# Attention with bit-shifted exponentials: GpSimd's shifts as packed 64-bit integer adds, two of three there, and other GpSimd work on VectorE

## The chip, the cores and the metric

The kernel runs on one core of a Trainium2 chip. Its engines run side by side, each with its own instruction stream in a fixed order: TensorE (PE in the profile; PEld are its weight loads), VectorE (DVE), ScalarE (ACT), GpSimd (POOL) and SyncE (SP), which issues nearly all DMAs. They meet through semaphores. The metric is the time of one execution in microseconds on the device; "the time" of a kernel is the median of several executions.

## The reference, cut to what matters

Inputs are bf16. S = 2048 rows, D = 512, 32 heads of 16, F = 1376.

```
def _A_ref(x, wqkv, wo):                       # attention
    qkv = (x @ wqkv).reshape(B, S, 3, 32, 16).transpose(2, 0, 3, 1, 4)
    q, k, v = qkv[0], qkv[1], qkv[2]
    scores = einsum("bhqd,bhkd->bhqk", q, k) * 16 ** -0.5
    o = einsum("bhqk,bhkd->bhqd", softmax(scores), v)
    return o.transpose(0, 2, 1, 3).reshape(B, S, D) @ wo

def _B_ref(x, w1, b1, w2, b2):                 # MLP over the row axis
    h = _layernorm(x)
    u = gelu(einsum("bsd,sf->bdf", h, w1) + b1)
    return (einsum("bdf,fs->bds", u, w2) + b2).transpose(0, 2, 1)

xn = _layernorm(x)
return x + _A_ref(xn, A_wqkv, A_wo) + _B_ref(xn, B_w1, B_b1, B_w2, B_b2)
```

So the input is normalised once, the attention works on that, and the MLP normalises it a second time.

## The kernel before

**Tiling.** Queries are cut into four blocks of 512, heads into eight groups of four. For each of 32 blocks (a query block with a group of heads), 16 key tiles of 128 and two halves of the group, there is one *n*: 1024 in all. For each n two matmuls (L691, 32 rows, 512 columns each) write scores into a slot of two PSUM banks; there are three slots. Then 128x1024 exponentials go into one of 28 buffers in SBUF (`pT`, 20 of them, and the space of the input `x_sb`, 8). Then the buffer is multiplied with V (L754), in groups of four matmuls of 256 columns, summed up in one PSUM bank. V carries a column of ones, so the same sum gives the softmax's denominators.

**Two ways to an exponential.** On ScalarE it is one `activation` (L715). On VectorE it is approximate: `dexp_spec` (L726) adds a bias to the scores and writes them as int16, whose bits, read as bf16, are a straight-line approximation of the exponential. Three copies of it, with 22, 58 and 94 added to the int16 bits (`SHIFTS`, written by `shift_spec`, L731), are further terms of a sum which is nearer to the true curve. The four terms are multiplied with V one after the other, the last with a scaled copy of V, `VM`, which `vm_scale` (L569) makes. An n that VectorE takes therefore costs one instruction at L726, three at L731 and four groups of matmuls at L754; one that ScalarE takes costs one instruction at L715 and one group.

**What sets the order.** The program text is made by a planner (`Sched` and the loop from L1201) with a modelled duration for each operation: `EXP_I, EXP_L` = 0.903, 1.03 for ScalarE's exponential, `P1_I, P1_L` = 1.13, 1.22 for VectorE's, `TS_I, TS_L` = 0.335, 0.42 for a shift on VectorE and `SH_I, SH_L` = 1.02, 1.08 for one on GpSimd (the first figure is until the next instruction, the second until the result). It repeatedly takes the candidate that can start first by the model and appends it to its engine's stream. What it fixed is the order on the chip, whatever the durations are there. It also decides which n go to VectorE: only while fewer than `D_FLY` = 3 such n have shifts still to be placed, while at least 8 buffers are free, and while VectorE's backlog is at most `D_BACK` = 0.5.

**Shifts.** The first of the three (k = 0) may go only to GpSimd until the scores run out; the second and third may go to either. The planner treats some operations of VectorE and GpSimd as users of one port (`port=True`, `port_time`): by its model they do not run at the same time. In the program a GpSimd operation waits by semaphore for the last such operation of VectorE ahead of it; in the other direction there is no semaphore.

**Other work on GpSimd.** Small operations of the first layernorm (L478, L480); the statistics of the second one (`ln2_stats`, L508 to L512) and its scaling of the 16 row tiles (`ln2_norm`, L516), both issued from the generator `h_work` in the main loop; `vm_scale`; and in each pair of blocks' epilogue two products of the head outputs with the reciprocal denominators (L981), 128x256 each.

**Around it.** The first block's 32 n go through a prologue of 16 periods, in which all exponentials are ScalarE's, and in which layernorm, transposes and the first projections run. During the main loop TensorE also computes the projections of later heads, the MLP (`ut`, `fin`, L784) and the output projection, and VectorE copies their results out of PSUM. ScalarE's gelu (L888) runs once.

Of the kernel before, what the change touches and what calls it, by code (L numbers as in the profile page):

```python
# [9 lines left out]
BF16 = mybir.dt.bfloat16  # L10
I16 = mybir.dt.int16
F32 = mybir.dt.float32

# [44 lines left out]
DMA_L = 3.5  # L58
SH_I, SH_L = 1.02, 1.08
D_LAST = 31  # L60
# [238 lines left out]
def bass_parallel_sum__softmax_full_mha__mixer_token_mlp__prompt_kernel(  # L299
# [18 lines left out]
    with ExitStack() as es:  # L318
# [196 lines left out]
        def ln2_norm(t):  # L515
            sc.add("pool", lambda e: e.tensor_scalar(xn_sb[:, t, :], xn_sb[:, t, :], mv[:, t, 3:4], 1.0, ALU.mult, ALU.mult),  # L516
                   reads=[("xn", t), ("mv", t)], writes=[("xn", t)], cost=(0.67, 0.75))

# [47 lines left out]

        def vm_scale(tiles, T):
            t0_, n = tiles[0], len(tiles)
            sc.add("pool", lambda e: e.tensor_scalar(  # L569
                vm_kh[:, t0_:t0_ + n, 8 * T:8 * T + 8, :], v17_kh[:, t0_:t0_ + n, 8 * T:8 * T + 8, :], CM, 1.0, ALU.mult, ALU.mult),  # L570
                reads=[("V", t, T) for t in tiles] + [("Vone",)], writes=[("VM", t, T) for t in tiles],
                cost=(0.62, 0.7))

# [130 lines left out]
        def buf_keys(i):  # L704
            return [("pT", i)] if i < NPB else [("pT", i), ("x", 2 * (i - NPB)), ("x", 2 * (i - NPB) + 1)]
# [23 lines left out]

        def shift_spec(eng, w, o, k):  # L730
            return dict(eng=eng, fn=lambda e: e.tensor_scalar(  # L731
                buf_i(o), buf_i(w), float(SHIFTS[k]), 1.0, ALU.add, ALU.mult),
                reads=[("pT", w)], writes=buf_keys(o), name="sh", port=True,
                cost=(SH_I, SH_L) if eng == "pool" else (TS_I, TS_L))

# [91 lines left out]
        def task_vt(T, j):  # L827
            tiles = list(range(4 * j, 4 * j + 4))
            for i, t in enumerate(tiles):
# [14 lines left out]
                reads=[("bank", EX_BANK)], writes=[("V", t, T) for t in tiles])]  # L844
            yield "call", lambda: (vm_scale(tiles, T), have.add(("v", T, j)))

# [92 lines left out]
        def task_epilogue(b):  # L939
# [39 lines left out]
            for h in range(2):  # L979
                cs = slice(256 * h, 256 * h + 256)  # L980
                yield "pool", [dict(eng="pool", fn=lambda e, cs=cs: e.tensor_tensor(  # L981
                    oT[0:m, qb % 2, T, cs], oC32[0:m, tb_, cs], denb[0:m, tb_, cs], ALU.mult),
                    reads=[("oC32", tb_, x, c, a) for x in es_ for c in range(4) for a in range(2)] +
                          [("denb", tb_, x, r) for x in es_ for r in range(4)],
                    writes=[("oTc", qb % 2, T), ("oTh", h)], port=True, cost=(0.68, 0.74))]
            yield "call", lambda: oT_done.add((qb, T))
# [79 lines left out]
        for period in range(NKT):  # L1066
# [10 lines left out]
            if period in VM_AT:  # L1077
                j = VM_AT.index(period)
                vm_scale(list(range(4 * j, 4 * j + 4)), 0)

        late_consts()
# [32 lines left out]
        hgen = h_work()  # L1114
        next_n = BN
# [3 lines left out]
        cur_ext = None  # L1119
        frees = [g_gelu]  # L1120
        pv_block = 0
        pv_open = True
        free_slots = [0, 1, 2]
        next_h = 0.0

# [72 lines left out]
        last_n = None  # L1198
        step_gen(g_gelu)
        fin_next = 0  # L1200
        while True:  # L1201
# [52 lines left out]
            if hgen is not None:  # L1254
                pl.append((max(sc.free["pool"], next_h), 2, "h", None, 0.67))
            pl = [z for z in pl if max(dve_port, sc.free["dve"]) - z[0] >= z[4] - PORT_SLACK]
# [51 lines left out]
            if not cands:  # L1308
                pl = [z for z in ([] if not sh_jobs else [(0, 0, "shd", (sh_jobs[0], shift_spec("dve", sh_jobs[0]["w"], sh_jobs[0]["o"], sh_jobs[0]["k"])))])]
                pl += [(0, 0, "gen", g) for g in frees if g["cur"] and g["cur"][0] == "pool"]  # L1310
                if hgen is not None:
                    pl.append((0, 0, "h", None))
# [7 lines left out]
            if kind == "h":  # L1320
                if next(hgen, "end") == "end":
                    hgen = None
            elif kind == "exp":
                n, sp_ = what
# [4 lines left out]
            elif kind == "dexp":  # L1329
# [74 lines left out]
            if cur_ext is None:  # L1404
                for i, (rel, due, nm, gen, need) in enumerate(ext_tasks):
                    if rel > next_n:
                        continue
                    if need and need[0] == "ut" and (need[1] != len(u_begun) or hgen is not None):
                        continue
# [73 lines left out]
```

## Time and profile before

| | |
|---|---|
| time, median of 5 runs | 715.37 us (713.55 to 716.51) |
| the profiled execution's own time | 713.55 us |
| its span from first to last instruction | 711.8 us |
| TensorE's granted clock | 1.00 in every stage |
| ScalarE's exponentials, L715 | 733 (522 into `pT`, 211 into `x_sb`) |
| VectorE's exponentials, L726 | 291 (201 and 90) |
| shifts on VectorE, L731 | 572 (284 + 131 + 111 + 46), 0.44 to 0.46 us each |
| shifts on GpSimd, L731 | 301 (149 + 73 + 59 + 20), 1.044 to 1.046 us each |
| head products on GpSimd, L981 | 32, 0.735 us each |
| second layernorm's scaling on GpSimd, L516 | 16, 0.720 us each |
| V scaling on GpSimd, L569 | 16, 0.662 us each |

From 40 to 690 us, the main loop, the engines are busy for 634.9 (TensorE), 616.7 (VectorE), 646.3 (ScalarE) and 354.9 us (GpSimd) of 650. A row of the profile gives busy time, mean length of one, and the idle time of the engine just before them with what ended it. Lengths overlap: an instruction's row reaches until its result is written, while the next one has begun; the distance from start to start is what an engine can do.

### The profile page before, as it was taken

To read this page: it belongs to the slowest core of one execution; us is meant where nothing else is said; L and a number is where in the kernel's file an instruction comes from. 1 tells how busy PE (TensorE), PEld (TensorE's weight loads), DVE (VectorE), ACT (ScalarE), POOL (GpSimd) and SP (SyncE) were. 2 spreads that over 40 slices of the span, in tenths; PEclk is the share of its full clock that TensorE was granted. 3 is DMA by queue.
4 is the path that set the end of the run, shared out by engine and by line. 5 is a ranking of instruction groups with operands and counts; after the bars stand their busy time and mean duration, and the time that the engine had idled before them with its cause. 6 is when DMAs were issued, how large, how long until landed. Compare 5 with 4: busy or idle time off the path is not lost.

```text
span 711.8 us, 28996 instructions
## 1 busy us (share of the span) xinstructions
PE 688.2 (97%) x12716; PEld 309.8 (44%) x12716; DVE 666.0 (94%) x1093; ACT 690.8 (97%) x752; POOL 383.6 (54%) x420
## 2 busy tenths in 40 slices
PE   8998999999999999999999999999999999999997
PEld 4544444444545444444444434444443434443443
DVE  7967999998999999999999999999999999999997
ACT  5999999999999999999999999999999999999994
POOL 5567554563545556464554554645554555645653
PEclk9999999999999999999999999999999999999999
DMA  7130022121202112221222211112221112212111
GB/s 209 29 74 20 21 46 43 27 42 25 49 10 49 31 36 54 46 44 34 49 52 44 58 36 38 38 45 49 51 48 27 46 43 51 62 25 61 34 25 43
DMA packets 85727, 32.29 MB, mean 45 GB/s; under 512 B 67425, under 2 KB 85601, under 8 KB 85601
## 3 DMA queue, kind: packets, MB, share of 16 engines
q1 hardware_dynamic: 85168, 30.05, 18.6%
q8 instruction: 99, 1.62, 1.0%
q10 hardware_dynamic: 432, 0.39, 0.2%
q14 instruction: 28, 0.22, 0.1%
HBM read 21.76 MB, written 2.35 MB: 34 GB/s over the span
## 4 chain that ended last, share of the span: by engine, by line
PE 44%; ACT 39%; DVE 14%; issue 2%; POOL 1%; DMA 1%; SPq 0%; DVEq 0%
ACT pT L715 28%; PE ps L754 16%; PE ps L691 15%; ACT x_sb L715 10%; PE ps L784 10%; DVE pT L726 5%; DVE pT L731 4%; DVE x_sb L726 2%; DVE x_sb L731 1%; PE ps L833 1%; ACT gT_sb L888 1%; DVE OT L944 1%; PE ps L597 1%; DMA x_sb<-in_A_x_dram 0%; PE ps L528 0%
## 5 line engine op out<-in xcount | busy, mean ns | idle before, releaser
L715 ACT ACTIVATE pT<-ps 128x1024 bf16<-128x1024 f32 x522 | 514.4, 1124 | 3.2 <-PE ps L691 1.8
L691 PE MATMUL ps<-QT,KT 32*128 32x512 bf16 x2048 | 288.0, 384 | 10.6 <-ACT pT L715 5.7
L726 DVE TENSOR_SCALAR pT<-ps 128x1024 int16<-128x1024 f32 x201 | 244.3, 1215 | 10.0 <-PE ps L691 9.1
L754 PE MATMUL ps<-pT,V 128*32 128x256 bf16 x4576 | 243.3, 275 | 3.7 <-DVE V L842 1.2
L715 ACT ACTIVATE x_sb<-ps 128x1024 bf16<-128x1024 f32 x211 | 227.4, 1134 | 1.7 <-PE ps L691 1.4
L731 POOL TENSOR_SCALAR pT<-pT 128x1024 int16<-128x1024 int16 x149 | 155.8, 1046 | 124.9 <-DVE pT L731 82.9
L691 PEld LDWEIGHTS ps<-QT,KT 32*128 32x128 bf16 x2048 | 79.3, 91 | 192.1 <-ACT pT L715 90.7
L754 PEld LDWEIGHTS ps<-pT,V 128*32 128x32 bf16 x4576 | 109.8, 96 | 82.7 <-issue 59.1
L731 DVE TENSOR_SCALAR pT<-pT 128x1024 int16<-128x1024 int16 x284 | 121.7, 451 | 3.2
L754 PE MATMUL ps<-x_sb,V 128*32 128x256 bf16 x1848 | 115.7, 275 | 0.7 <-POOL x_sb L731 0.4
L726 DVE TENSOR_SCALAR x_sb<-ps 128x1024 int16<-128x1024 f32 x90 | 109.5, 1216 | 6.1 <-PE ps L691 5.8
L731 POOL TENSOR_SCALAR pT<-x_sb 128x1024 int16<-128x1024 int16 x73 | 76.2, 1044 | 62.4 <-DVE pT L731 47.8
L731 POOL TENSOR_SCALAR x_sb<-pT 128x1024 int16<-128x1024 int16 x59 | 61.6, 1044 | 53.3 <-DVE pT L731 37.0
L754 PE MATMUL ps<-pT,VM 128*32 128x256 bf16 x864 | 61.3, 275 | 1.6 <-POOL VM L569 1.5
L754 PEld LDWEIGHTS ps<-x_sb,V 128*32 128x32 bf16 x1848 | 47.4, 96 | 30.4 <-issue 22.7
L784 PE MATMUL ps<-gT_sb,wblk 128*32 128x512 bf16 (+1 forms) x704 | 58.4, 384 | 0.6 <-DVE Qall L806 0.6
L731 DVE TENSOR_SCALAR pT<-x_sb 128x1024 int16<-128x1024 int16 x131 | 57.2, 459 | 1.5
L784 PE MATMUL ps<-hx,wblk 128*32 128x512 bf16 x688 | 56.9, 382 | 0.0
L731 DVE TENSOR_SCALAR x_sb<-pT 128x1024 int16<-128x1024 int16 x111 | 50.0, 458 | 1.2
L981 POOL TENSOR_TENSOR oT<-oC,denb 128x256 bf16<-128x256 f32 (+1 forms) x32 | 23.5, 735 | 26.9 <-DVE pT L731 20.0
L731 POOL TENSOR_SCALAR x_sb<-x_sb 128x1024 int16<-128x1024 int16 x20 | 20.9, 1044 | 20.0 <-DVE pT L731 17.1
L754 PEld LDWEIGHTS ps<-pT,VM 128*32 128x32 bf16 x864 | 22.9, 96 | 14.0 <-issue 10.0
(103 smaller groups left out, 409.9 us busy)
## 6 DMA issues: line engine op xcount, KB each, us to landing
wblk<-in_B_w_dram SPq DMA_DIRECT2D x10, 512.0 KB, 4.5
wblk<-in_B_w_dram SPq DMA_DIRECT2D x16, 320.0 KB, 3.6
oC<-OT SPq DMA_DIRECT2D x248, 16.0 KB, 1.8
denb<-rden_scratch SPq DMA_DIRECT2D x124, 32.0 KB, 1.9
xr<-in_A_x_dram SPq DMA_DIRECT2D x16, 128.0 KB, 2.5
dcomp<-OT SPq DMA_DIRECT2D x124, 2.0 KB, 1.8
QT<-Qall SPq DMA_DIRECT2D x120, 16.0 KB, 1.8
out_dram<-osb SPq DMA_DIRECT2D x14, 128.0 KB, 2.0
```

What stands on the lines that cost most here:

```text
L597: sc.add("pe", lambda e: e.matmul(bank(bk), lhsT=src[:, 0:128], rhs=src, start=True, stop=True), reads=keys, writes=[("bank", bk)], cost=( ...
L691: specs.append(dict(eng="pe", fn=lambda e, r=r, bk=bk: e.matmul(bank(bk), lhsT=KT[32 * r:32 * r + 32, T, 128 * kt:128 * (kt + 1)], rhs=QT[ ...
L715: return [dict(eng="act", fn=lambda e: e.activation(buf(pbuf[n]), ps[:, s_ * 1024:(s_ + 1) * 1024], ACTF.Exp, scale=LN2_128), reads=[("ban ...
L726: return dict(eng="dve", fn=lambda e: e.tensor_scalar(buf_i(w), ps[:, s_ * 1024:(s_ + 1) * 1024], IBIAS, 0.0, ALU.add, ALU.max), reads=[(" ...
L731: return dict(eng=eng, fn=lambda e: e.tensor_scalar(buf_i(o), buf_i(w), float(SHIFTS[k]), 1.0, ALU.add, ALU.mult), reads=[("pT", w)], writ ...
L754: specs.append(dict(eng="pe", fn=lambda e, c=c, h=h, i=i, off=off: e.matmul(bank(PV_BANK)[32 * c:32 * c + 32, 256 * par:256 * par + 256], ...
L784: specs.append(dict(eng="pe", fn=lambda e, c=c, w=w: e.matmul(bank(EX_BANK)[32 * c:32 * c + w, :], lhsT=lhs_of(32 * c, 32 * c + w), rhs=rh ...
L833: specs.append(dict(eng="pe", fn=lambda e, ct=ct, c=c, i=i, t=t: e.matmul(bank(EX_BANK)[32 * c:32 * c + 32, 128 * i:128 * (i + 1)], lhsT=x ...
L888: yield "act", [dict(eng="act", fn=lambda e, ap=ap: e.activation(ap, ap, ACTF.Gelu_apprx_tanh), reads=[("gT", f) for f in fts], writes=[(" ...
L944: yield "pvev", [dict(eng="dve", fn=lambda e: e.tensor_copy(OT32[:, eb, :], bank(PV_BANK)), reads=[("bank", PV_BANK)], writes=[("OT32", eb)])]
L981: yield "pool", [dict(eng="pool", fn=lambda e, cs=cs: e.tensor_tensor(oT[0:m, qb % 2, T, cs], oC32[0:m, tb_, cs], denb[0:m, tb_, cs], ALU. ...
```

## The change

GpSimd's shifts become `int64_add` on the same buffers seen as 256 64-bit integers per partition, with the shift repeated in each of the four 16-bit fields. The planner's cost for them falls to 0.62, 0.70. Of the three shifts, the third may go to VectorE at once, the second only if GpSimd is 0.3 us behind VectorE by the model, the first as before.

The head products (L981), the second layernorm's scaling and the V scaling of head groups 1 to 3 are issued on VectorE. `ln2_stats` stays on GpSimd and is issued in period 13 of the prologue. The V scaling of head group 0 stays on GpSimd in the prologue. After the prologue's last constants GpSimd has nothing but shifts.

```
-SH_I, SH_L = 1.02, 1.08
+SH_I, SH_L = 0.62, 0.70
+HN_I, HN_L = 0.20, 0.29
...
         def ln2_norm(t):
-            sc.add("pool", lambda e: e.tensor_scalar(xn_sb[:, t, :], xn_sb[:, t, :], mv[:, t, 3:4], 1.0, ALU.mult, ALU.mult),
-                   reads=[("xn", t), ("mv", t)], writes=[("xn", t)], cost=(0.67, 0.75))
+            return [dict(eng="dve", fn=lambda e: e.tensor_scalar(xn_sb[:, t, :], xn_sb[:, t, :], mv[:, t, 3:4], None, ALU.mult),
+                         reads=[("xn", t), ("mv", t)], writes=[("xn", t)], cost=(HN_I, HN_L), port=True)]
...
-        def vm_scale(tiles, T):
+        def vm_scale(tiles, T, eng="pool"):
             t0_, n = tiles[0], len(tiles)
-            sc.add("pool", lambda e: e.tensor_scalar(
+            sc.add(eng, lambda e: e.tensor_scalar(
                 vm_kh[:, t0_:t0_ + n, 8 * T:8 * T + 8, :], v17_kh[:, t0_:t0_ + n, 8 * T:8 * T + 8, :], CM, 1.0, ALU.mult, ALU.mult),
                 reads=[("V", t, T) for t in tiles] + [("Vone",)], writes=[("VM", t, T) for t in tiles],
-                cost=(0.62, 0.7))
+                cost=(0.62, 0.7) if eng == "pool" else (HN_I, HN_L), port=True)
...
         def shift_spec(eng, w, o, k):
+            if eng == "pool":
+                return dict(eng=eng, fn=lambda e: e.int64_add(
+                    buf_i(o).bitcast(I64), buf_i(w).bitcast(I64), SHIFTS[k] * 0x0001000100010001),
+                    reads=[("pT", w)], writes=buf_keys(o), name="sh", port=True, cost=(SH_I, SH_L))
...
-            yield "call", lambda: (vm_scale(tiles, T), have.add(("v", T, j)))
+            yield "call", lambda: (vm_scale(tiles, T, "dve"), have.add(("v", T, j)))
...
-                yield "pool", [dict(eng="pool", fn=lambda e, cs=cs: e.tensor_tensor(
+                yield "dve", [dict(eng="dve", fn=lambda e, cs=cs: e.tensor_tensor(
                     oT[0:m, qb % 2, T, cs], oC32[0:m, tb_, cs], denb[0:m, tb_, cs], ALU.mult),
...
-                    writes=[("oTc", qb % 2, T), ("oTh", h)], port=True, cost=(0.68, 0.74))]
+                    writes=[("oTc", qb % 2, T), ("oTh", h)], port=True, cost=(0.33, 0.41))]
...
+            if period == 13:
+                ln2_stats()
...
-        def h_work():
-            ln2_stats()
+        def task_h():
             for t in range(NT):
-                ln2_norm(t)
-                sc.last_writer[("h", t)] = sc.last_writer[("xn", t)]
-                sc.readers[("h", t)] = []
-                yield
+                yield "dve", ln2_norm(t)
+                yield "call", lambda t=t: h_mark(t)
...
-                    sh_jobs.append(dict(n=n, w=w, o=o, k=k, ok=lambda k=k: k > 0 or (next_n >= NN and not ready_q)))
+                    sh_jobs.append(dict(n=n, w=w, o=o, k=k, ok=lambda k=k: k > 1 or (k > 0 and sc.free["pool"] > sc.free["dve"] + 0.3) or (next_n >= NN and not ready_q)))
```

`h_mark` holds the two bookkeeping lines that `h_work` had, and the loop's conditions on `h_work` being finished become conditions on all 16 tiles being marked.

More of the change, by code (lines that the diff above doesn't have):

```diff
@@ L11 @@
 I16 = mybir.dt.int16
+I64 = mybir.dt.int64
 F32 = mybir.dt.float32
@@ L58 @@
 DMA_L = 3.5
-SH_I, SH_L = 1.02, 1.08
+SH_I, SH_L = 0.62, 0.70
+HN_I, HN_L = 0.20, 0.29
+OT_I, OT_L = 0.60, 0.685
 D_LAST = 31
@@ L733, in shift_spec @@
                 reads=[("pT", w)], writes=buf_keys(o), name="sh", port=True,
-                cost=(SH_I, SH_L) if eng == "pool" else (TS_I, TS_L))
+                cost=(TS_I, TS_L))
         def add(spec):
@@ L1103, in bass_parallel_sum__softmax_full_mha__mixer_token_mlp__prompt_kernel, with h_mark @@
         ext_tasks.sort(key=lambda z: z[1])
-        def h_work():
-            ln2_stats()
+        def h_mark(t):
+            sc.last_writer[("h", t)] = sc.last_writer[("xn", t)]
+            sc.readers[("h", t)] = []
+            h_done.append(t)
+        def task_h():
             for t in range(NT):
-                ln2_norm(t)
-                sc.last_writer[("h", t)] = sc.last_writer[("xn", t)]
-                sc.readers[("h", t)] = []
-                yield
+                yield "dve", ln2_norm(t)
+                yield "call", lambda t=t: h_mark(t)
+        h_done = []
         g_gelu = dict(gen=task_gelu(), cur=None)
-        hgen = h_work()
         next_n = BN
@@ L1119, in bass_parallel_sum__softmax_full_mha__mixer_token_mlp__prompt_kernel @@
         cur_ext = None
-        frees = [g_gelu]
+        g_h = dict(gen=task_h(), cur=None)
+        frees = [g_gelu, g_h]
         pv_block = 0
@@ L1123, in bass_parallel_sum__softmax_full_mha__mixer_token_mlp__prompt_kernel @@
         free_slots = [0, 1, 2]
-        next_h = 0.0
         def step_gen(g):
@@ L1199, in bass_parallel_sum__softmax_full_mha__mixer_token_mlp__prompt_kernel @@
         step_gen(g_gelu)
+        step_gen(g_h)
         fin_next = 0
@@ L1253, in bass_parallel_sum__softmax_full_mha__mixer_token_mlp__prompt_kernel @@
                     pl.append((est(g["cur"][1]), 0, "gen", g, 1.25))
-            if hgen is not None:
-                pl.append((max(sc.free["pool"], next_h), 2, "h", None, 0.67))
             pl = [z for z in pl if max(dve_port, sc.free["dve"]) - z[0] >= z[4] - PORT_SLACK]
@@ L1310, in bass_parallel_sum__softmax_full_mha__mixer_token_mlp__prompt_kernel @@
                 pl += [(0, 0, "gen", g) for g in frees if g["cur"] and g["cur"][0] == "pool"]
-                if hgen is not None:
-                    pl.append((0, 0, "h", None))
                 if not pl:
@@ L1319, in bass_parallel_sum__softmax_full_mha__mixer_token_mlp__prompt_kernel @@
                 fill(t_est, kind == "score" and t_est <= sc.pe_end - 0.05)
[L1320 to L1323, printed above, removed]
+            if kind == "exp":
                 n, sp_ = what
@@ L1407, in bass_parallel_sum__softmax_full_mha__mixer_token_mlp__prompt_kernel @@
                         continue
-                    if need and need[0] == "ut" and (need[1] != len(u_begun) or hgen is not None):
+                    if need and need[0] == "ut" and (need[1] != len(u_begun) or len(h_done) < NT):
                         continue
```

## The prediction

> **What bounds the kernel now.** I read the page first: span, busy shares and the chain of waits.
>
> ```profile
> span 711.8 us, 28996 instructions
> PE 688.2 (97%) x12716; PEld 309.8 (44%) x12716; DVE 666.0 (94%) x1093; ACT 690.8 (97%) x752; POOL 383.6 (54%) x420
> ...
> PE 44%; ACT 39%; DVE 14%; issue 2%; POOL 1%; DMA 1%; SPq 0%; DVEq 0%
> ```
>
> Three engines are full; GpSimd (POOL) is not. The chain names TensorE most, so I next read who waited for whom (total us, times, longest):
>
> ```profile
> POOL pT L731 <- DVE pT L731: 130.7, 132, 4.2
> ...
> PEld ps L691 <- ACT pT L715: 90.7, 314, 0.8
> ...
> PEld ps L691 <- ACT x_sb L715: 37.3, 129, 0.8
> ...
> DVE pT L726 <- PE ps L691: 9.1, 21, 2.3
> ```
>
> The weights of the score matmuls (L691) wait 128 us for ScalarE to give a PSUM bank back, while VectorE's exponential waits 9 us for scores and ScalarE's 3.2 (in the first group below; 1.7 more in its x_sb group). TensorE follows; the 1024 exponentials, split between ScalarE and VectorE, set the pace. The groups of instructions give the split:
>
> ```profile
> L715 ACT ACTIVATE pT<-ps 128x1024 bf16<-128x1024 f32 x522 | 514.4, 1124 | 3.2 <-PE ps L691 1.8
> L726 DVE TENSOR_SCALAR pT<-ps 128x1024 int16<-128x1024 f32 x201 | 244.3, 1215 | 10.0 <-PE ps L691 9.1
> L731 POOL TENSOR_SCALAR pT<-pT 128x1024 int16<-128x1024 int16 x149 | 155.8, 1046 | 124.9 <-DVE pT L731 82.9
> L731 DVE TENSOR_SCALAR pT<-pT 128x1024 int16<-128x1024 int16 x284 | 121.7, 451 | 3.2
> L981 POOL TENSOR_TENSOR oT<-oC,denb 128x256 bf16<-128x256 f32 (+1 forms) x32 | 23.5, 735 | 26.9 <-DVE pT L731 20.0
> ```
>
> With the x_sb groups beside them: 522 + 211 = 733 exponentials on ScalarE, 201 + 90 = 291 on VectorE. Each of the 291 needs three shifted copies: 873 in all, 301 on GpSimd (149 + 73 + 59 + 20) and 572 on VectorE, so about one and two. How the two share time shows in the timeline (start, length):
>
> ```profile
> 300.63 1.22 DVE L726 TENSOR_SCALAR pT<-ps 128x1024 int16<-128x1024 f32 x1
> 301.89 0.43 DVE L731 TENSOR_SCALAR pT<-pT 128x1024 int16<-128x1024 int16 x1
> 302.23 1.22 DVE L726 TENSOR_SCALAR pT<-ps 128x1024 int16<-128x1024 f32 x1
> 303.36 0.42 DVE L731 TENSOR_SCALAR pT<-pT 128x1024 int16<-128x1024 int16 x1
> 303.69 0.42 DVE L731 TENSOR_SCALAR x_sb<-pT 128x1024 int16<-128x1024 int16 x1
> ```
>
> ```profile
> 300.88 1.04 POOL L731 TENSOR_SCALAR pT<-x_sb 128x1024 int16<-128x1024 int16 x1 [0.96 <-DVE pT L731]
> ...
> 310.67 2.17 POOL L731 TENSOR_SCALAR pT<-pT 128x1024 int16<-128x1024 int16 x2 [0.69 <-DVE pT L731]
> ```
>
> A VectorE exponential gives way to the next instruction after 1.13 us (302.23 to 303.36), but after 1.26 where GpSimd still works (300.63 to 301.89: GpSimd ended at 301.92). A VectorE shift and a GpSimd operation exclude each other; the exponential, which reads PSUM, runs beside GpSimd. So GpSimd has the time under exponentials and PSUM copies, no more. A GpSimd shift takes 1.045 with 0.08 between two (2.17 for two).
>
> **The model of before.** ScalarE starts an exponential every 0.91 us (four starts in its timeline, 302.34 to 305.07). With d exponentials on VectorE the span is T = 45 + 0.91 (1024 - d); the 45 is what is left of 712 at d = 291 (start, end, gelu, waits). VectorE: mean start to start is 1.215 from an exponential and 0.38 from a shift over the whole timeline, so 291 x 1.215 + 572 x 0.38 = 571, and 141 remain (layernorm, PSUM copies, start, end, idle): T = 141 + d (1.215 + 2 x 0.38).
>
> **The change, part by part.**
>
> Shifts: two of three go to GpSimd, as the second is VectorE's only when GpSimd lies 0.3 us behind. VectorE's price k for one exponential falls from 1.975 to 1.215 + 0.38 = 1.595 if GpSimd keeps out of its way. At 0.43 us a GpSimd shift hides wholly under the exponential: 1.13 + 0.38 = 1.51.
>
> The 64-bit add has no row. It handles 256 elements of 8 bytes. Lower bound: per element, as int16. The rows 128x1024 (1.045) and 128x544 (L569, 0.662) give 0.80 ns an element and 0.23 fixed: 0.23 + 0.20 = 0.43. Upper bound: per byte, 1.045 as now. I take 0.66: the nearest rows by elements are L981's, which write 256 per partition in 0.735 but read two tensors, so one input should be less. The planner's own 0.62 to 0.70 in the diff fits: its figures for the GpSimd operations that the trace does show (0.62 to 0.70 for L569, 0.68 to 0.74 for L981) hold their rows.
>
> Moved to VectorE: 32 head products. Nearest row: the tail's product L1018, same shape, 0.425 long, some 0.34 start to start: 11 us. 16 layernorm scalings, as L500 (same shape, 0.449 long, 0.36 start to start): at most 6. 12 V scalings of 544 elements, 0.20 to 0.36 each: 2 to 4. Together 18 to 21; I take 20, all of it on the bound engine, hidden by nothing. 141 becomes 161. The statistics of the second layernorm (L512, 2.96 us, and three small ones) stay on GpSimd but move ahead of the loop, where GpSimd idles 4.9 us before L569 at 39.3; nothing reads them soon: nothing. If that cover were missing, about 4 us. No DMA is added or moved. The three moved kinds no longer stand in GpSimd's queue, where L981 alone waited 26.9 us.
>
> New wait: VectorE behind GpSimd. Per exponential the pair needs the shared access for 2 x (0.66 + 0.08) + 0.38 = 1.86, where VectorE itself needs 1.51. If GpSimd got in only under exponentials, k would be 1.86. But PSUM copies and other VectorE work, some 110 us in the loop or 0.35 per exponential, let GpSimd through too. k lies between 1.51 and 1.86; I take the middle, 1.70. Behind a late shift stand the next exponential on VectorE, then the PSUM bank, then the scores.
>
> Sum: 45 + 0.91 (1024 - d) = 161 + 1.70 d gives **d = 313 and a span of 692 us**; k = 1.51 gives 670, k = 1.86 gives 709. Is TensorE able? An exponential on VectorE is multiplied with V four times instead of once. TensorE's timeline gives 0.11 for such a group of four matmuls (x4 0.28, x8 0.39, x12 0.51), 0.43 for a score with its two changes of mode, 0.44 for two scores together. I count 307 single and 352 double: 287, plus 1897 groups x 0.11 = 209, plus 513 groups of L784 at 0.215 = 110, plus some 32 for L833 and the start: 638 of 712. 22 more exponentials add 22 x 3 x 0.11 = 7: 645 under 692, so it hides, at the cost of 27 us less spare time.
>
> The profiled run took 713.55 for its span of 711.8, and the median is 715.37: 3.6 from span to median. **692 + 3.6 = 696.**
>
> The Trainium skill (Perfetto Trace Analysis, Optimizing Scalar/DVE Operations) warns that moving work between VectorE and GpSimd might not help, since they share an SBUF port under an exclusive lock. The trace shows the lock (301.89 above) but also GpSimd idle for 46% of the span; by that rule the change would give nothing, 715, by the rows 696. GPSIMD Engine Reference, section 2.1 (Instruction dispatch), states about 6 us at the first call of freshly loaded GpSimd code; no run here shows it, and were it all on the path the sum would be 702.
>
> **Rivals.**
>
> 1. *The add is slow.* The order is fixed ahead with the planner's 0.62, so a slower add is not balanced again. At x us it makes the port the bound: 313 (2 (x + 0.08) + 0.38) + 70 (50 of start and end, 20 moved). This passes 712 at x = 0.755, and at 1.045 the span is 893. For it: bytes may count, and 64-bit carries are more work than a fused int16 pair; against it: the element slope and the 0.735 row with two inputs. Slower than before; chance 0.15.
> 2. *TensorE does not keep up.* Its spare time is latency from bank to weights. If all 74 us stay, 645 + 74 = 719, 723 as a median; below 47 it does not decide. For it: PE 97% and 44% of the chain; against it: it waits for ScalarE, and can double more scores. I put it at about 709; chance 0.16, half of it still faster.
> 3. *The add is cheap*, near 0.43: 670 to 680, 674 to 684 as a median; chance 0.10.
> 4. *The plan does not raise d*, as three exponentials in flight and 28 buffers limit it: ScalarE keeps 733, time stays at about 715; chance 0.07.
>
> **How the numbers follow.** The forecast, 684 to 713 as a median (k = 1.60 to 1.86), has 0.52. About 0.3% can be told from no change here: 713.2 to 717.5. Faster: 0.52 + 0.10 + 0.08 = 0.70; same: 0.05 from rival 2 and 0.04 from 4, 0.09; slower: 0.15 + 0.03 + 0.03 = 0.21. The range runs from 679, half into rival 3, to 721, over rivals 2 and 4 and the add up to about 0.77; the rest of rival 1 is left out.
>
> **What would show it.** GpSimd's L731 rows near 0.66, twice as many as VectorE's; L726 near 313, L715 near 711; exponential to shift on VectorE longer than 1.215 in the mean, and ending where GpSimd ends; GpSimd above 60% busy. Wrong: an add above 0.75 with VectorE's shifts held, L726 still at 291, or waits of L715 for L691 far above 5 us.

## The result: 0.3% slower, and the profile after

| | before | changed |
|---|---|---|
| time, median | 715.11 us (712.41 to 718.61, 47 runs) | 717.27 us (715.66 to 719.07, 26 runs) |
| ratio | | 1.0027 [1.0017, 1.0037] |
| span of the profiled execution | 711.8 us | 715.5 us |
| exponentials on ScalarE / VectorE | 733 / 291 | 720 / 304 |
| shifts on VectorE / GpSimd | 572 / 301 | 322 / 590 |

The forecast was 696 us and faster. The change made the kernel slightly slower: the interval lies above 1, though the median is inside the 713.2 to 717.5 us that the prediction had called no change. The page after, its span, its busy shares and its chain of waits by engine:

```profile
span 715.5 us, 29352 instructions
PE 689.2 (96%) x12867; PEld 314.8 (44%) x12867; DVE 623.0 (87%) x916; ACT 678.6 (95%) x739; POOL 382.0 (53%) x649
...
PE 67%; ACT 19%; DVE 7%; issue 3%; SPq 2%; POOL 1%; DMA 1%; DVEq 0%; POOLq 0%
```

VectorE lost 43 us of work (666.0 to 623.0), and the span did not become shorter. The groups of instructions after (busy us, mean ns of one, idle time just before them):

```profile
L718 ACT ACTIVATE pT<-ps 128x1024 bf16<-128x1024 f32 x522 | 510.4, 1125 | 9.6 <-PE ps L694 8.5
L729 DVE TENSOR_SCALAR pT<-ps 128x1024 int16<-128x1024 f32 x216 | 263.9, 1222 | 27.8 <-PE ps L694 20.4
L735 POOL INT64_ADD pT<-pT x311 | 188.4, 613 | 158.9 <-DVE pT L738 91.1 <-DVE x_sb L738 34.0 <-PE ps L694 19.5
L718 ACT ACTIVATE x_sb<-ps 128x1024 bf16<-128x1024 f32 x198 | 211.8, 1128 | 3.8 <-PE ps L694 3.3
L729 DVE TENSOR_SCALAR x_sb<-ps 128x1024 int16<-128x1024 f32 x88 | 107.6, 1222 | 10.1 <-PE ps L694 7.2
L738 DVE TENSOR_SCALAR pT<-pT 128x1024 int16<-128x1024 int16 x154 | 65.6, 428 | 4.6
```

The 64-bit add takes 0.613 us, near the 0.66 of the sum. But VectorE now stands idle before its exponentials for 37.9 us (27.8 + 10.1; 16.1 before), and ScalarE for 13.4 (9.6 + 3.8; 4.9 before): both wait for scores. VectorE has less to do and waits longer, so it does not hold the changed kernel up; whether it did before is asked below.

More than half of ScalarE's added wait of 8.5 us (13.4 - 4.9) is one place:

```profile
247.05 1.02 ACT L718 ACTIVATE pT<-ps 128x1024 bf16<-128x1024 f32 x1 [4.58 <-PE ps L694]
```

From 241.1 to 246.6 us TensorE's timeline has no score matmul; in its fixed order it multiplies with V and computes projections of later heads (L791, L840). Before, the longest such wait in the loop was 0.46 us.

The start shows something that no step of the forecast had in its sum. GpSimd's first instructions before, in the timeline (start, length, and in brackets the idle time before it with what ended it):

```profile
0.72 0.20 POOL L392 MEMSET ident<- 128x128 bf16 x1 [0.29 <-POOLq L1468]
1.17 0.29 POOL L393 TENSOR_SCALAR_AFFINE_SELECT ident<-ident 128x128 bf16<-128x128 bf16 x1 [0.24 <-POOL ident L392]
```

and after, with two later ones:

```profile
0.72 0.20 POOL L395 MEMSET ident<- 128x128 bf16 x1 [0.29 <-POOLq L1474]
8.54 0.28 POOL L396 TENSOR_SCALAR_AFFINE_SELECT ident<-ident 128x128 bf16<-128x128 bf16 x1 [7.62 <-issue]
...
49.15 0.24 POOL L468 CAST b1col<-b1c_bf 128x11 f32<-128x11 bf16 x1
56.77 0.61 POOL L735 INT64_ADD pT<-x_sb  x1 [7.39 <-DVE pT L738]
```

The very same selection waits 7.62 us for nothing that the profile shows. `mhalf` and `qmask` stand behind it in GpSimd's queue. ScalarE's timeline after:

```profile
8.91 0.20 ACT L603 ACTIVATE rcomp<-mhalf 128x1 f32<-128x1 f32 x1 [5.98 <-POOL qmask L409]
...
19.44 3.78 ACT L718 ACTIVATE pT<-ps 128x1024 bf16<-128x1024 f32 x4 [0.48 <-PE ps L694]
```

ScalarE's `rcomp` waits 5.98 us for them, with the rest of ScalarE's start behind it. Before, the first exponential on ScalarE began at 12.08; now at 19.44, 7.4 us later. (In the runs below where the selection does not wait so long, this start lies between 11.3 and 13.1 us, so the 7.4 is good to about 1 us.)

A second idle stretch, 7.39 us, stands before the first 64-bit add, but that one is a wait for data. VectorE's first exponential ends at 56.20, the shift behind it (first line below) at 56.66, and the add starts 0.11 us later. In `moves`, a run described below that has no 64-bit add, GpSimd's first shift waits even longer in the same place (second line):

```profile
56.23 0.43 DVE L738 TENSOR_SCALAR pT<-x_sb 128x1024 int16<-128x1024 int16 x1
```

```profile
51.29 1.05 POOL L734 TENSOR_SCALAR pT<-x_sb 128x1024 int16<-128x1024 int16 x1 [8.63 <-DVE VM L572]
```

From ScalarE's first exponential to the end of the span it was 699.7 us before (711.8 - 12.08) and is 696.1 now (715.5 - 19.44): all that follows the start won 3.6 us, and the start lost 7.4.

So the span nearly closes with three terms: 13 fewer exponentials on ScalarE, 13 x 0.91 = -11.8; the late start, +7.4; and ScalarE's longer wait for scores, 13.4 - 4.9 = +8.5. The sum is +4.1, measured +3.7.

### The profile page after: what moved, and what is told of

The parts are those of the page before. It is cut to its first block, busy times and chain, and to the rows that moved or that the text cites. A ratio compares the mean times of both kernels' runs of the same rounds, so it can differ in the third digit from the quotient of the medians.

```text
span 715.5 us, 29352 instructions
## 1 busy us (share of the span) xinstructions
PE 689.2 (96%) x12867; PEld 314.8 (44%) x12867; DVE 623.0 (87%) x916; ACT 678.6 (95%) x739; POOL 382.0 (53%) x649
## 4 chain that ended last, share of the span: by engine, by line
PE 67%; ACT 19%; DVE 7%; issue 3%; SPq 2%; POOL 1%; DMA 1%; DVEq 0%; POOLq 0%
PE ps L761 26%; PE ps L694 24%; PE ps L791 14%; ACT pT L718 13%; ACT x_sb L718 5%; SPq L391 2%; DVE pT L729 2%; PE ps L840 1%; DMA denb<-rden_scratch 1%; DVE x_sb L729 1%; DVE hx L519 1%; ACT gT_sb L895 1%; DVE OT L951 1%; DVE pT L738 0%; DVE oT L988 0%
## 5 line engine op out<-in xcount | busy, mean ns | idle before, releaser
L729 DVE TENSOR_SCALAR pT<-ps 128x1024 int16<-128x1024 f32 x216 | 263.9, 1222 | 27.8 <-PE ps L694 20.4
L735 POOL INT64_ADD pT<-pT x311 | 188.4, 613 | 158.9 <-DVE pT L738 91.1
L718 ACT ACTIVATE x_sb<-ps 128x1024 bf16<-128x1024 f32 x198 | 211.8, 1128 | 3.8 <-PE ps L694 3.3
L729 DVE TENSOR_SCALAR x_sb<-ps 128x1024 int16<-128x1024 f32 x88 | 107.6, 1222 | 10.1 <-PE ps L694 7.2
L735 POOL INT64_ADD pT<-x_sb x117 | 71.2, 616 | 55.8 <-DVE pT L738 40.4
L735 POOL INT64_ADD x_sb<-pT x113 | 69.1, 613 | 57.5 <-DVE pT L738 34.3
L738 DVE TENSOR_SCALAR pT<-pT 128x1024 int16<-128x1024 int16 x154 | 65.6, 428 | 4.6
L791 PE MATMUL ps<-gT_sb,wblk 128*32 128x512 bf16 (+1 forms) x704 | 60.4, 384 | 0.5 <-ACT gT_sb L895 0.3
L791 PE MATMUL ps<-hx,wblk 128*32 128x512 bf16 x688 | 59.8, 389 | 0.0
L735 POOL INT64_ADD x_sb<-x_sb x49 | 30.0, 616 | 26.9 <-DVE pT L738 15.2
L738 DVE TENSOR_SCALAR x_sb<-pT 128x1024 int16<-128x1024 int16 x70 | 29.7, 427 | 1.9
L738 DVE TENSOR_SCALAR pT<-x_sb 128x1024 int16<-128x1024 int16 x70 | 29.6, 426 | 1.8
L761 PE MATMUL ps<-x_sb,VM 128*32 128x256 bf16 x352 | 25.3, 275 | 0.0
```

The costliest lines, as they stand in the source:

```text
L718: return [dict(eng="act", fn=lambda e: e.activation(buf(pbuf[n]), ps[:, s_ * 1024:(s_ + 1) * 1024], ACTF.Exp, scale=LN2_128), reads=[("ban ...
L729: return dict(eng="dve", fn=lambda e: e.tensor_scalar(buf_i(w), ps[:, s_ * 1024:(s_ + 1) * 1024], IBIAS, 0.0, ALU.add, ALU.max), reads=[(" ...
L735: return dict(eng=eng, fn=lambda e: e.int64_add(buf_i(o).bitcast(I64), buf_i(w).bitcast(I64), SHIFTS[k] * 0x0001000100010001), reads=[("pT ...
L738: return dict(eng=eng, fn=lambda e: e.tensor_scalar(buf_i(o), buf_i(w), float(SHIFTS[k]), 1.0, ALU.add, ALU.mult), reads=[("pT", w)], writ ...
L761: specs.append(dict(eng="pe", fn=lambda e, c=c, h=h, i=i, off=off: e.matmul(bank(PV_BANK)[32 * c:32 * c + 32, 256 * par:256 * par + 256], ...
L791: specs.append(dict(eng="pe", fn=lambda e, c=c, w=w: e.matmul(bank(EX_BANK)[32 * c:32 * c + w, :], lhsT=lhs_of(32 * c, 32 * c + w), rhs=rh ...
```

## The experiments

**First question: what is the 7.4 us at the start?** My theory was that GpSimd keeps code for a set of operations, that the 64-bit add and the ordinary ones lie in different sets, and that an execution starts with what the last one left. Then one tiny ordinary operation at the end, behind the last shift, should move the gap to where nothing waits for GpSimd. It works on columns of `mv` that nothing reads any more.

```
+sc.add("pool", lambda e: e.tensor_tensor(mv[:, 0:1, 2], mv[:, 0:1, 1], mhalf[:], ALU.mult),
+       reads=[("mv", 0), ("mhalf",)], writes=[("mv", 0)], cost=(0.2, 0.3))
```

> The changed kernel with one small GpSimd tensor product added behind GpSimd's last shift, which brings GpSimd's ordinary code back before the end. Theory: the 7.4 us that the changed kernel's first GpSimd selection (L396) loses at the start is a code load, paid because the previous execution ended with the 64-bit add's code resident; here the load falls under the tail, so ScalarE's first exponential starts at 12.1 instead of 19.4 us and the time is 7 to 8 us under the changed kernel's, about 710. Rival: the load at the start comes whatever was resident, or the one at the end holds the final barrier: 717, as the changed kernel.

It took 707.61 us (before on the same chip 713.46), ratio 0.9918 [0.9902, 0.9933]. GpSimd's timeline in this kernel, the start, the first 64-bit add and the end:

```profile
1.41 0.29 POOL L396 TENSOR_SCALAR_AFFINE_SELECT ident<-ident 128x128 bf16<-128x128 bf16 x1 [0.49 <-POOL ident L395]
...
50.28 0.61 POOL L735 INT64_ADD pT<-x_sb  x1 [7.39 <-DVE pT L738]
...
693.38 0.61 POOL L735 INT64_ADD pT<-pT  x1 [0.61 <-DVE x_sb L738]
701.15 0.18 POOL L1059 TENSOR_TENSOR mv<-mv,mhalf 128x1 f32<-128x1 f32 x1 [7.15 <-issue]
```

The gap has left the start and now stands at the end, 7.15 us, under the output's last steps. ScalarE's first exponential begins at 12.98. One instruction of 0.18 us thus makes the changed kernel 1.1% faster (0.9918 against 1.0027), and this version beats the kernel before. All nine runs that end with it show the same: the selection waits 0.49 us, and a stretch of 6.99 to 7.79 us stands before the last operation. So what GpSimd ran last in one execution decides whether the next one waits at its start. That the time goes into loading code is inferred: the profile shows no instruction in the stretch. The stretch before the first add, at 50.28, is as long as before, as a wait for data would be; a load into the adds, if there is one, could lie under it.

**Second question: which engine sets the pace of the loop?** The forecast had VectorE and ScalarE as equal bounds. I took r_restore with its order of instructions unchanged and made one engine's work shorter at a time; each of these leaves work out. r_act: ScalarE's exponentials of the loop do 976 of 1024 columns. r_dve: VectorE's exponentials do 928 of 1024. r_pe: the matmuls of the fourth term with V are left out, except for a block's first and last groups.

```
r_act
-    fn=lambda e: e.activation(buf(pbuf[n]), ps[:, s_ * 1024:(s_ + 1) * 1024],
+    fn=lambda e, w=1024 if n < BN else 976: e.activation(buf(pbuf[n], 0, w), ps[:, s_ * 1024:s_ * 1024 + w],
r_dve
-    buf_i(w), ps[:, s_ * 1024:(s_ + 1) * 1024], IBIAS, 0.0, ALU.add, ALU.max),
+    buf_i(w)[:, 0:928], ps[:, s_ * 1024:s_ * 1024 + 928], IBIAS, 0.0, ALU.add, ALU.max),
r_pe
+    grp = [add(s_) for s_ in pv_specs(item, first, pv_left[b] == 0)]
+    if term == len(SHIFTS) and not first and pv_left[b] > 0:
+        dropped.extend(grp)
...
+    sc.streams["pe"] = [op for op in sc.streams["pe"] if id(op) not in gone]
```

> As r_restore in every order and plan, but ScalarE's exponentials in the loop work on 976 of 1024 columns, some 0.04 us less each, 27 us in all; the last 48 columns keep older values. Theory (TensorE paces): at most 5 us less. Rival (ScalarE paces): 15 to 27 us less.

> As r_restore in every order and plan, but VectorE's exponentials work on 928 of 1024 columns, 0.10 us less each, 30 us in all; the last 96 columns keep older values. Theory (TensorE paces): at most 3 us less, as VectorE already idles for 90 us. Rival (VectorE with the port, as forecast): 10 to 25 us less.

> As r_restore in every order and plan, but the matmuls of the fourth term with V (some 300 groups of 0.11 us, 33 us of TensorE's time) are left out of the program, so the result lacks that term. Theory: after the change TensorE paces the loop, with ScalarE close behind (720 exponentials x 0.91 + 45 = 700 us), so the span falls by about 8 and up to that floor. Rival, VectorE with GpSimd on their port, as forecast: no more than 2 us.

| same chip | us | against r_restore | what became shorter |
|---|---|---|---|
| r_restore | 707.61 | | |
| r_act | 696.41 | -11.2 | ScalarE's busy time, 677.7 to 657.9 |
| r_dve | 705.69 | -1.9 | VectorE's busy time, 622.6 to 596.0 |
| r_pe | 705.61 | -2.0 | 1212 matmuls fewer (12867 to 11655); TensorE's busy time, 687.2 to 679.5 |

Their ratios to the kernel before are 0.9761 [0.9738, 0.9784], 0.9891 [0.9868, 0.9914] and 0.9890 [0.9865, 0.9915]. Where VectorE's shorter work went can be read in r_dve's groups:

```profile
L718 ACT ACTIVATE pT<-ps 128x1024 bf16<-128x1024 f32 x522 | 509.6, 1123 | 9.1 <-PE ps L694 8.1
L729 DVE TENSOR_SCALAR pT<-ps 128x928 int16<-128x928 f32 x216 | 242.3, 1122 | 41.9 <-PE ps L694 40.1
...
L729 DVE TENSOR_SCALAR x_sb<-ps 128x928 int16<-128x928 f32 x88 | 98.8, 1123 | 15.7 <-PE ps L694 14.7
```

Each exponential is 0.1 us shorter (1122 against 1222 ns) and VectorE's idle time before its exponentials grows from 36.3 in r_restore (26.8 + 9.5) to 57.6 us. The time from an exponential's start to the shift behind it fell with it, from 1.256 to 1.156, so GpSimd did not use the saving up. ScalarE's row is as it was. VectorE does not bound the changed kernel.

My theory at this point was that TensorE did; r_pe's 2 us speak against it, with the reserve that the 33 us of its expectation are an estimate. In r_act 11.2 of ScalarE's 19.8 us reached the time, and its idle time before its exponentials grew from 11.3 to 19.7 us, which is the rest. The chains that ended last, r_act first and r_pe below, show which engine is next:

```profile
PE 82%; DVE 9%; ACT 4%; SPq 2%; DMA 1%; issue 1%; POOL 1%; DVEq 0%; POOLq 0%
```

```profile
ACT 62%; PE 26%; DVE 6%; issue 2%; POOL 2%; SPq 1%; DMA 0%; DVEq 0%; POOLq 0%
```

ScalarE sets most of the pace here, and TensorE seems to stand close behind it: where ScalarE is shortened the chain lies on TensorE. No run shortens both, so how close is not known.

**Was VectorE the bound before the change?** The same cuts in the kernel before (edits as above, at L715, L726 and in the emission of L754):

> The kernel before, same plan, with ScalarE's exponentials in the loop on 976 of 1024 columns (27 us of ScalarE's time; the last 48 columns keep older values). The forecast's model: ScalarE and VectorE both set the pace, so shortening one alone brings under half of what it saves: 5 to 12 us. If ScalarE alone paces: over 15.

> The kernel before, same plan, with VectorE's exponentials on 928 of 1024 columns (29 us of VectorE's time; the last 96 columns keep older values). The forecast's model: VectorE is as tight as ScalarE: 5 to 12 us. If VectorE was never the bound: under 3 us, as in the changed kernel.

> The kernel before, same plan and order, with the matmuls of the fourth term with V left out (some 290 groups, 32 us of TensorE's time; the result lacks that term). If TensorE paced the kernel before: 10 to 20 us less. If ScalarE does, as shortening it brought 5.5 us and shortening VectorE 2: at most 5 us.

| | us | before, same chip | ratio |
|---|---|---|---|
| b_act | 709.02 | 714.53 | 0.9922 [0.9897, 0.9946] |
| b_dve | 712.44 | 714.53 | 0.9980 [0.9965, 0.9995] |
| b_pe | 711.29 | 715.05 | 0.9952 [0.9937, 0.9968] |

The page of b_dve, its busy line:

```profile
PE 685.9 (97%) x12711; PEld 308.1 (43%) x12716; DVE 646.3 (91%) x1093; ACT 689.4 (97%) x752; POOL 384.3 (54%) x420
```

VectorE has 19.7 us less to do (666.0 to 646.3) and the kernel is 2.1 us faster: a tenth. The rest became idle time of VectorE (span less busy time: 45.8 before, 64.0 here). ScalarE's 17.4 us less (690.8 to 673.4 in b_act) gave 5.5, a third; TensorE's cut gave 3.8. VectorE at 94% busy was therefore not the bound before either, and no single engine was it wholly; ScalarE's exponentials come nearest.

**Third question: why not more exponentials on VectorE?** If VectorE has room, the plan should give it more. `D_STEAL` is the constant of the planner that decides when VectorE may take the only ready score ahead of ScalarE; at 0 the plan gives VectorE 350. r_steal_pe is the same with the fourth term's matmuls left out as in r_pe, to see whether TensorE's time for 46 more four-fold scores is what costs.

```
-D_STEAL = 0.8
+D_STEAL = 0.0
```

> As r_restore, but the planner lets VectorE take the only ready score without a condition (D_STEAL 0 in place of 0.8), so the plan gives VectorE 350 exponentials in place of 304. The forecast's model (ScalarE and VectorE share the exponentials, nothing else counts): ScalarE needs 45 + 0.91 x 674 = 658, VectorE 161 + 1.7 x 350 = 756, so about 756, with VectorE full and ScalarE idle. Theory (supply of scores): ScalarE and VectorE both idle, both waiting for scores from TensorE, which itself waits for PSUM banks; time 715 to 725, waits of L718 and L729 for L694 far above the 12 and 27 us of r_restore.

> As r_steal (350 exponentials on VectorE), same plan and order, with the matmuls of the fourth term with V left out (some 345 groups x 0.11 = 38 us of TensorE's time; the result lacks that term). Theory (TensorE's own time holds the scores back when VectorE gets more exponentials): 20 to 35 us under r_steal's 728, ScalarE's 60 us of waiting for scores more than halved. Rival (the three pairs of PSUM banks: a score waits for a bank, not for TensorE): within 8 us of r_steal.

r_steal took 727.59 (before 714.53), 1.0181 [1.0161, 1.0202]; r_steal_pe 721.30 (before 715.05), 1.0095 [1.0065, 1.0124]. The groups of r_steal:

```profile
L718 ACT ACTIVATE pT<-ps 128x1024 bf16<-128x1024 f32 x482 | 468.2, 1047 | 49.5 <-PE ps L694 48.5
...
L718 ACT ACTIVATE x_sb<-ps 128x1024 bf16<-128x1024 f32 x192 | 195.1, 1053 | 11.0 <-PE ps L694 10.8
```

ScalarE has 46 exponentials less (674), some 42 us at 0.91, and stands idle 60.5 us before its exponentials, 49 more than in r_restore (11.3). The forecast's 756 is far off; my theory's 715 to 725 is missed too, and of its two idle engines only ScalarE came: VectorE's idle time before its exponentials fell, from 36.3 to 21.2 us. r_steal_pe is 6 us faster, within the rival's 8, and ScalarE still waits 54.5 (44.5 + 10.0) in it, with most of the fourth term's matmuls left out. So the wait is mostly not TensorE's time for the multiplications. The next two runs ask about the scores' slots, but in r_restore's order; in r_steal's own order that was not tried.

**Is it the way of a score through its PSUM slot?** r_sc cuts the score matmuls to 384 of 512 columns from the third block on, so TensorE is shorter and each slot is filled sooner. r_act_dve makes both cuts in the exponentials at once, so that every slot is also emptied sooner.

```
r_sc
+    w = 512 if n < 2 * BN else 384
-    bank(bk), lhsT=KT[32 * r:32 * r + 32, T, 128 * kt:128 * (kt + 1)],
-    rhs=QT[32 * r:32 * r + 32, b % 4, :], start=True, stop=True,
+    bank(bk)[:, 0:w], lhsT=KT[32 * r:32 * r + 32, T, 128 * kt:128 * (kt + 1)],
+    rhs=QT[32 * r:32 * r + 32, b % 4, 0:w], start=True, stop=True,
```

> As r_restore in every order and plan, but from the 65th score on a score matmul streams 384 of 512 columns (the other columns of its bank keep older values): 0.053 us less for each of some 630 score groups, 33 us of TensorE's time, as much as r_pe took away (which brought 2 us). Theory (each score's way through its pair of PSUM banks holds the loop: matmul, exponential, release): the 0.053 is on that way, 960 x 0.053 / 3 pairs = 17 us, so 8 to 17 us under r_restore. Rival (the order, with ScalarE, holds it, and TensorE's time is hidden anyway): as r_pe, about 2 us.

> As r_restore, with both cuts of r_act (27 us of ScalarE) and r_dve (30 us of VectorE), which brought 11 and 2 us alone. Theory (each score's way through its banks): both cuts shorten it, the sum or more, 13 to 20 us. Rival (ScalarE alone, at 720 exponentials): 11 us as r_act.

r_sc: 706.31 (before 713.53), 0.9892 [0.9844, 0.9940], which cannot be told from r_pe and is short of the 8 to 17 us that the theory of the slots wanted. r_act_dve: 695.64, 0.9743 [0.9678, 0.9807], which cannot be told from r_act alone, but its interval is too wide to rule out the theory's 13 us. So r_sc speaks against the theory that the way through the slots sets the pace, and r_act_dve decides nothing. In the order of r_restore ScalarE's own work alone moves the time by more than 2 us.

**The parts of the change alone.** "moves" has the changed kernel's moved operations, but int16 shifts on GpSimd (1.02, 1.08 in the plan) under the old rule of one in three. b_tuned is the kernel before, and r_tuned is r_restore, each with the planner's constants set anew. All three also stop the planner's filling matmuls once the last `fin` tile is done.

```
moves
-SH_I, SH_L = 0.62, 0.70
+SH_I, SH_L = 1.02, 1.08
-    if eng == "pool":
-        return dict(eng=eng, fn=lambda e: e.int64_add(
...
-ok=lambda k=k: k > 1 or (k > 0 and sc.free["pool"] > sc.free["dve"] + 0.3) or ...
+ok=lambda k=k: k > 0 or ...
r_tuned
-D_FLY = 3
-D_BACK = 0.5
-D_STEAL = 0.8
-D_LATE = 0.6
-P_KEEP = 4
-PORT_SLACK = 0.5
+D_FLY = 4
+D_BACK = 0.8
+D_STEAL = 1.0
+D_LATE = 1.4
+P_KEEP = 5
+PORT_SLACK = 0
...
```

> The changed kernel without its 64-bit adds: GpSimd's shifts are int16 at 1.02 as before, one of three goes to GpSimd as before, but layernorm scaling, V scaling and head products are on VectorE. No other GpSimd code is needed, so no load at the start. Forecast's model: 20 us more on a bound VectorE: +20 / 2 or about 725. Theory (VectorE was no bound): 714 to 720, the plan's own difference.

> The kernel before with the planner's constants set anew in the same way as in r_tuned (D_LATE 1.4, D_BACK 0.9, PORT_SLACK 0.2, PE_FIT 0.02, KV_STEP 16, UT_STEP 36, UT_DUE 96, UT_LEAD 14, SH_I 1.06), to tell what of r_tuned's 700 is the setting and what the change. Theory: 708 to 713, so that the change with its load hidden is worth 8 to 12 us between two tuned plans. Rival (the setting alone does it): 698 to 703.

> r_restore with the planner's constants set anew for the new shift costs (D_LATE 1.4, D_STEAL 1.0, D_BACK 0.8, DEAD_SLACK 0, P_KEEP 5, D_FLY 4, PORT_SLACK 0, KV_STEP 12, UT_STEP 40, UT_DUE 104, Q_LEAD 58, 0.8 for the threshold of the second shift, SH_I 0.60); VectorE gets 305 exponentials, as before the re-setting, but with scores earlier and fewer single scores. Theory (supply of scores in the plan's order holds ScalarE and VectorE): 697 to 703, 5 to 10 us under r_restore. Rival (ScalarE's 719 exponentials are the floor already): within 2 us of r_restore.

| | us | before, same chip | ratio | on VectorE |
|---|---|---|---|---|
| moves | 715.63 | 715.05 | 1.0020 [1.0003, 1.0036] | 288 |
| b_tuned | 710.82 | 715.05 | 0.9943 [0.9923, 0.9963] | 288 |
| r_tuned | 700.33 | 714.53 | 0.9792 [0.9776, 0.9807] | 305 |

The moves, with the stopped filling matmuls, cost 0.2%. From there to r_restore, that is the packed adds, their share of two in three and the plan that follows from them (with the filling matmuls back), it is 0.9918 / 1.0020 = 0.990: 1.0% won. The wait at the start costs 1.1%. Those three make the result. r_tuned is the best version seen. Its page and groups:

```profile
span 701.3 us, 29291 instructions
PE 682.5 (97%) x12875; PEld 321.0 (46%) x12880; DVE 611.7 (87%) x902; ACT 675.4 (96%) x738; POOL 391.2 (56%) x668
...
L719 ACT ACTIVATE pT<-ps 128x1024 bf16<-128x1024 f32 x503 | 489.0, 1085 | 7.5 <-PE ps L695 6.5
...
L719 ACT ACTIVATE x_sb<-ps 128x1024 bf16<-128x1024 f32 x216 | 223.9, 1086 | 3.0 <-PE ps L695 3.0
```

It has almost as many exponentials on ScalarE as the changed kernel (719 and 720), and its span of 701.3 is near 45 + 0.91 x 719 = 699, ScalarE's equation. (The execution took 703.08; the median is lower.) That equation is no floor, though: for b_tuned, with 736, it gives 715, and the span was 710.8. Its 45 holds waits and an end that another plan can shorten. Between two kernels that each have their constants set anew, the change with its last GpSimd operation is worth about 0.9792 / 0.9943 = 0.985, 1.5%. How far each setting was searched is not on record, so a part of that can be the setting.

## Why the prediction was wrong, step by step

**The failed step is the balance.** "45 + 0.91 (1024 - d) = 161 + 1.70 d gives d = 313" treats VectorE's line as a bound that the plan would use up to the end. b_dve shows that it was none: a tenth of what VectorE saves reaches the time. A sign stood in the page of before: the prediction read 9 us of waiting for scores on VectorE, but with the second group of its exponentials its idle time before them was 16.1 us (10.0 + 6.1), against ScalarE's 4.9. The 141 of "T = 141 + 1.975 d" was found by subtraction from the span, so it held VectorE's waits as if they were need. After the change the same line, with the k that was measured, stands far below the span: exponential to shift is 1.256 in the mean, and 322 / 304 = 1.06 shifts of 0.38 make k = 1.66, so 161 + 1.66 x 304 = 666 of 715.5. Nothing pulls the two lines together: the planner decides by its own constants how many exponentials VectorE gets, and with D_STEAL at 0 it gives 350 and the kernel is slower (r_steal). The moves that were "hidden by nothing" cost 0.2%: at the 288 of "moves" VectorE's line gives 161 + 1.975 x 288 = 730, ScalarE's 45 + 0.91 x 736 = 715, and the profiled span is 716.4 (that execution took 718.24, the median is 715.63). The packed adds do win time, but why the plan with them wins 1.0% is not shown beyond its 16 fewer exponentials on ScalarE.

**ScalarE's line held.** The difference between forecast and span has three terms: d came to 304 and not 313, 9 x 0.91 = 8.2; the start is late by 7.4; ScalarE waits 8.5 longer for scores. 692 + 24.1 = 716, measured 715.5. ScalarE's waits, 13.4 us, are one of the signs of being wrong that the prediction named. The first term is the failed balance. The second was missing from the sum, and it alone turned the sign: without it, r_restore's 707.61 is faster and inside the forecast's 684 to 713. Of the third, 4.6 us are the one place ahead of 247.05 us where the order has no score for ScalarE, which no term of the equations holds.

**The code load was named and left out.** The Trainium skill (GPSIMD Engine Reference, section 2.1, Instruction dispatch) gives about 6 us for the first call of freshly loaded code. The trace shows 7.62 us, if that is the same thing, on the way back from the adds to the ordinary operations, which falls into the next execution's start; on the way into the adds no run here shows it apart from the wait for data. In the profile of before there was no such gap to see, and I did not ask which code GpSimd holds when an execution ends. The price behind that sentence, 702, would still have been faster than before.

**The sizes.** The add: 0.613 to 0.616 against 0.66 taken, inside 0.43 to 1.045. Head products 13.7 us and layernorm scaling 6.2 as busy time, with the V scaling within reach of the 20. GpSimd at 53% stayed below the 60% that I had named: the adds were shorter, and 590 instead of 626.

**The wait of VectorE behind GpSimd was misread.** k came to 1.66 (with the 0.38 of before), near the forecast's 1.70, but by luck. The prediction held that a VectorE exponential gives way after 1.13 us alone and after 1.26 beside GpSimd. In its own window GpSimd's next shift runs until 303.44, and yet VectorE's shift begins at 303.36, 1.13 after its exponential:

```profile
302.40 1.04 POOL L731 TENSOR_SCALAR pT<-pT 128x1024 int16<-128x1024 int16 x1 [0.48 <-DVE pT L731]
```

Over the whole timeline of the changed kernel the step is 1.256 in the mean both where GpSimd is at work 1.08 us into the exponential (151 times) and where it is idle (110). What the step goes by is what the shift reads. Where the tiles' names (`pT`, `x_sb`) show that it reads an older exponential's output, it is 1.14 (38 times before, with GpSimd at work in 36). In the changed kernel it starts 0.03 us after the end of the exponential just ahead, and where r_dve shortens that by 0.10 the step is 0.10 shorter. The timeline of the changed kernel, VectorE first and GpSimd below, shows such a shift begin at 308.40, while two adds end only at 308.53:

```profile
306.73 0.43 DVE L738 TENSOR_SCALAR pT<-pT 128x1024 int16<-128x1024 int16 x1
307.14 1.23 DVE L729 TENSOR_SCALAR x_sb<-ps 128x1024 int16<-128x1024 f32 x1
308.40 0.43 DVE L738 TENSOR_SCALAR pT<-x_sb 128x1024 int16<-128x1024 int16 x1
```

```profile
307.33 1.20 POOL L735 INT64_ADD pT<-pT  x2 [1.11 <-DVE pT L738]
308.93 0.61 POOL L735 INT64_ADD pT<-x_sb  x1 [0.40 <-DVE pT L738]
```

GpSimd does shut a shift of VectorE out, but it shows in the length of the shift. Before, VectorE first and GpSimd below:

```profile
689.61 1.08 DVE L731 TENSOR_SCALAR pT<-pT 128x1024 int16<-128x1024 int16 x1
```

```profile
689.37 1.04 POOL L731 TENSOR_SCALAR x_sb<-x_sb 128x1024 int16<-128x1024 int16 x1
```

GpSimd ends at 690.41, and VectorE's shift 0.28 us later. All 48 shifts above 0.46 us before and all 18 after end 0.28 us after a GpSimd operation. Against a usual length of 0.425 VectorE lost 18.6 us to this before and 1.3 after; the mean shift into `pT` fell from 451 to 428 ns. So the forecast's new wait, (1.70 - 1.595) x 313 = 33 us, did not come, and the 301.89 that the prediction named was no sign of the shared access.

**The Trainium skill's rule that offloading might not help** (Perfetto Trace Analysis, Optimizing Scalar/DVE Operations), taken as no gain, gave 715 and stood nearer than my 696, but not for its reason: GpSimd did take 590 shifts, and VectorE lost 1.3 us by it; only little waited for the work that left VectorE.

**The rivals.** Rival 4, that the plan hardly raises d, is the nearest: 304 where it had 291 and I 313. I gave it 0.07. That the time also came near its 715 is luck, as it takes the 7.4 us at the start, which it did not hold. Its reason is refuted: r_steal reaches 350 with the same three in flight and the same buffers, so D_STEAL held d at 304. Rival 1 did not come: the add of 64-bit numbers took 0.613 us, less than the 1.045 of the int16 add. Rival 2 has its symptom, ScalarE waiting for scores and TensorE at 67% of the chain, but r_pe and r_sc, which take TensorE's work away, give about 2 us; that TensorE would be next behind ScalarE, as r_act's chain says, is open.

**Left open.** What in the order makes ScalarE wait for scores as soon as VectorE is given more, r_steal's 60 us, is not settled: TensorE's time for the multiplications does not explain it, and the slots were tried only in r_restore's order. That TensorE's queue has a fixed order, so that one late shift holds the scores behind it, is an idea only. A version whose GpSimd work all lies in one set of code was not tried.

## What to carry to other kernels

A busy share of 94% and a line fitted to the span do not make an engine the bound: make its work shorter by a few per cent in an unchanged order and see how much of it reaches the time, before costing a change that frees it. After a change of prices set the planner's constants anew on both sides before comparing; here that was worth 0.6% to the kernel before (0.9943) and 1.3% to r_restore (0.9918 to 0.9792). When a GpSimd operation of another kind comes in, look at the first and last GpSimd instructions of an execution, and lead it back to the ordinary code where nobody waits.

## What the runs showed of the hardware that I had not expected

What GpSimd ran last outlives the execution: the wait of 7.62 us at an instruction that before took 0.24 to come to was set by the last instruction of the execution before it, and one 0.18 us operation at the end removed it. In the profile it is an idle stretch put down to "issue" (7.15 and 7.62 us). A stretch of the same length with a releaser, as the 7.39 us "<-DVE" ahead of the first add, can be something else, so the releaser's own time has to be looked at: here it ended 0.11 us before the add. A VectorE shift that starts well inside a GpSimd operation shows the wait in its own length and ends 0.28 us after that operation (all 48 longer than 0.46 us before, all 18 after). The 64-bit add on 256 elements takes 0.613 us where the int16 add on the same bytes took 1.045: its time goes neither by elements alone (0.43 by the slope of before) nor by bytes.
